# Attention and a feed-forward pair in one kernel: v times p of two head pairs in one run on TensorE, and a new order of work

## The chip, the cores and the metric

The kernel runs on 1 core of one Trainium2 chip. The metric is the device time of one launch in microseconds (us). The kernel before takes 998.44 us, the median of 3 runs (998.38 to 999.49).

## What is computed

Eight batches of eight heads, 576 tokens, head size 64, block-causal attention with blocks of 64 tokens; then a feed-forward layer with SiLU over all 4608 tokens:

```python
def _attn_ref(q, k, v):
    scores = 1/sqrt(64) * q @ k.T
    scores = where(pos_i // 64 >= pos_j // 64, scores, -1e9)
    scores = scores - max(scores)
    attn = exp(scores)
    attn = attn / (sum(attn) + 1e-9)
    return attn @ v

x = attn_out.transpose(0, 2, 1, 3).reshape(4608, 512)
h = x @ w_in                      # 512 x 2048
out = (h * sigmoid(h)) @ w_out    # 2048 x 512
```

All data are float32.

## The kernel before

**The order is written out.** A string, `ORDER`, lists some 4500 tokens, one for each step: `u20.scores`, `w3.bits:0`, `ffn`. The loop at L1196 calls the method that a token names, and each engine then runs its instructions in the order in which the tokens stand. Tile pools insert the waits. So where a step stands among the steps of its own engine decides when it can run.

**Names.** `a`, `b` (class First) are the first 64 query rows of all heads, `c0` to `c3` (Second) the next 64; `u0` to `u63` (Unit) are one head each, of the remaining 448 query rows. `w0` to `w15` are pieces of W_in, `o0` to `o15` pieces of W_out, `t0` to `t7` (Turned) pieces of W_out in the seven-product form below. `ffn` is the next half-step of x times W_in (ffn1), `keep` and `save` bring its result h through SBUF to DRAM. `i0` to `i71` (Item) read h back, apply SiLU and split it; `y0` to `y17` (Out) are the 18 output blocks of 256 rows, four items each. `warm:n` are matmuls of zeros. In `a`, `b` and `c`, `norm` divides p by its sum and `turn` transposes p on PE ahead of their `pv`.

**Precision.** Each float32 factor is split into a rounded fp32r part (`hi`, ScalarE) and the rest (`lo`, VectorE or GpSimd), and three fp32r matmuls make one product. Only v times p (`Unit.pv`, L800) is done with unsplit float32. Weights arrive as 64-bit words; `rebias` (ScalarE), `sign` (GpSimd, the first four W_in pieces) and `bits` (VectorE, through PSUM bank "C") turn them into float32.

**A unit.** `split_hi`, `split_q` and `split_k` (ScalarE and others) split q and k ahead of it. `scores` (L702) fills three of four PSUM banks. `max`, `gather`, `top`, `spread`, `wide` find and broadcast the row maximum, `sub` and `exp` make p. Units go in pairs: `pv` of the odd unit multiplies v of both heads with their p, one head to each half of PE's columns, ten matmuls in five widths into bank `U`. Then `inverse`, `mult` (U times the inverse sum), `x_hi`, `x_lo` make one 128-row piece of x. p has three buffers (`p{u.i % 3}`, L753).

**The stages.** From the start to some 100 us: `a`, `b`, `c` and the weights. To some 565 us: the units, with `ffn` half-steps between them on PE. Then the rest of `ffn`, while t3 to t7 are made. Last, the products `prod` of 18 blocks: seven half-size products in place of eight (`PRODUCTS`), added up by `Out.add` (L1143, VectorE) from four PSUM banks, which the next block's products fill again. t0 to t2 lie in the pool `ta` (NTA = 3) and are made among the units.

Of the kernel before, what the change touches and what calls it, by code (L numbers as in the profile page):

```python
# [72 lines left out]
c0.scores:0 b.back:0 b.turn:1 w5.rebias w1.lo w2.bits:0 w4.rebias ffn c0.max:0 b.back:1 w3.sign w2.bits:2 c0.exp:0 w9.load b.pv
w3.bits:0 c0.scores:1 w10.load all.mask b.hi:0 w3.bits:2 b.hi:1 ffn w2.hi c0.max:1 c3.load_v w3.hi w2.lo b.lo:0 c0.exp:1 b.lo:1
w4.bits:0 w3.lo ffn c0.sum w6.rebias c1.load w4.bits:1 w7.rebias c0.norm w4.bits:2 ffn keep w11.load w8.rebias w5.bits:0 w4.hi
save c0.turn:0 w5.bits:1 keep w4.lo c3.scores:0 w12.load c0.back:0 w5.bits:2 o1.rebias c0.turn:1 c3.max:0 w5.hi ffn save w6.bits:0
c0.back:1 w5.lo c3.exp:0 w6.bits:1 w13.load c0.pv w6.bits:2 c3.scores:1 c0.hi c1.load_v w7.bits:0 w6.hi ffn c0.lo w10.rebias
w14.load w6.lo c3.max:1 w9.rebias w7.bits:1 c3.exp:1 c1.scores:0 w7.bits:2 ffn c1.max:0 w15.load keep c3.sum c1.exp:0 save
w8.bits:0 c3.norm ffn w8.bits:1 w7.hi w8.bits:2 c1.scores:1 keep w7.lo w9.bits:0 c3.turn:0 w11.rebias save c1.max:1 w8.hi c2.load
ffn w9.bits:1 c3.back:0 w8.lo c1.exp:1 w9.bits:2 c3.turn:1 ffn w10.bits:0 c3.back:1 c1.sum w10.bits:1 w9.hi c1.norm c3.pv keep  # L80
w10.bits:2 w12.rebias ffn save w11.bits:0 w10.hi w9.lo w13.rebias w11.bits:1 c1.turn:0 o0.rebias w11.bits:2 ffn w10.lo c1.back:0
w12.bits:0 w11.hi w14.rebias c1.turn:1 w12.bits:1 w11.lo ffn c1.back:1 w12.bits:2 keep w13.bits:0 w15.rebias save c1.pv w12.hi
w13.bits:1 ffn w12.lo c1.hi c2.load_v w13.bits:2 c1.lo w13.hi c2.scores:0 w14.bits:0 keep w13.lo w14.bits:1 save ffn u0.load
c2.max:0 w14.bits:2 c2.exp:0 ffn w15.bits:0 w15.bits:1 w14.hi c2.scores:1 w15.bits:2 keep w14.lo ffn save c2.max:1 w15.hi u1.load
o0.bits:0 w15.lo all.staged c2.exp:1 ffn o0.bits:1 o0.bits:2 u0.split_hi ffn c2.sum o2.load o1.bits:0 c2.norm keep o1.bits:1
t0.hi:0 ffn save o1.bits:2 u0.split_q t0.hi:1 o3.load c2.turn:0 keep ffn u0.split_k c2.back:0 save c2.turn:1 ffn u2.load t0.x:0
c2.back:1 t0.x:1 c2.pv t0.hi:2 keep t0.x:2 u0.load_v ffn c2.hi save t0.lo:0 c3.hi u2.load_v c2.lo t0.hi:3 u3.load_v t0.lo:2 ffn
c3.lo u1.load_v t0.lo:3 u0.scores keep u0.max:0 t0.lo:1 save u0.max:1 ffn u1.split_hi u0.max:2 o2.rebias ffn u1.split_q u0.gather
o2.bits:0 o3.rebias u1.split_k u0.top ffn o2.bits:1 u0.spread u0.wide keep u3.load ffn u0.sub:0 u0.sub:1 save u0.exp:0 u1.scores
u0.sub:2 u0.exp:1 u0.exp:2 u1.max:0 ffn u1.max:1 u2.split_hi u0.add:0 u1.max:2 keep ffn u2.split_q u0.sums:0 u1.gather save  # L90
o2.bits:2 u0.add:1 u1.top ffn u1.spread o4.load o3.bits:0 u2.split_k u1.wide keep t1.hi:0 ffn u0.sums:1 save u1.sub:0 u4.load
t1.lo:0 u1.sub:1 u1.exp:0 u2.scores keep u1.sub:2 u1.exp:1 save u2.max:0 ffn u1.exp:2 u2.max:1 u3.split_hi u1.add:0 u2.max:2 u1.pv
u3.split_q u1.sums:0 u2.gather o3.bits:1 u2.top u3.split_k o3.bits:2 u2.spread ffn o5.load t1.hi:1 u2.wide u5.load u1.add:1
u2.sub:0 u2.sub:1 u3.scores t1.x:0 u2.exp:0 u4.load_v keep u3.max:0 u5.load_v u2.exp:1 save u1.sums:1 t1.x:1 ffn u4.split_hi
u3.max:1 t1.x:2 u3.max:2 t1.hi:2 ffn u4.split_q t1.hi:3 u2.sub:2 u3.gather u4.split_k ffn u1.sums_x u2.exp:2 u3.top u2.sums:0
u3.spread ffn u6.load u1.sums_g u2.add:0 u3.wide keep u3.sub:0 u2.add:1 u3.sub:1 save u4.scores u3.exp:0 keep u4.max:0 u1.sums_m
u3.exp:1 u2.sums:1 save ffn u5.split_hi u3.sub:2 u4.max:1 u5.split_q u3.exp:2 ffn u4.max:2 u3.add:0 ffn u1.inverse keep u4.gather
u1.mult save u3.add:1 u3.pv u4.top u3.sums:0 u4.spread u5.split_k u3.sums:1 u1.x_hi u4.wide u3.sums_x u4.sub:0 u7.load u1.x_lo
u3.sums_g u4.sub:1 u5.scores u4.exp:0 u6.load_v u4.sub:2 u3.sums_m u4.exp:1 u7.load_v u5.max:0 u4.exp:2 ffn u5.max:1 u6.split_hi
u4.add:0 u5.max:2 ffn keep u3.inverse u6.split_q u5.gather save ffn u5.top u3.mult u5.spread u4.add:1 u4.sums:0 u3.x_hi u5.wide  # L100
u6.split_k ffn keep u4.sums:1 save u5.sub:0 ffn u5.sub:1 u8.load u3.x_lo u5.exp:0 u5.sub:2 u5.exp:1 t1.lo:3 u6.scores u5.exp:2
u6.max:0 keep u5.add:0 u6.max:1 u5.pv save u7.split_hi u6.max:2 u5.add:1 u5.sums:0 u6.gather u7.split_q u5.sums:1 u6.top ffn
u5.sums_x u8.load_v u6.spread u7.split_k u9.load_v u5.sums_g u6.wide ffn u6.sub:0 u9.load u5.sums_m u6.sub:1 u6.exp:0 u7.scores
u6.sub:2 u6.exp:1 u6.exp:2 u7.max:0 t1.lo:1 u7.max:1 ffn keep u8.split_hi save u7.max:2 u6.add:0 ffn o5.rebias u5.inverse
u8.split_q u7.gather u5.mult ffn keep u7.top u6.add:1 u6.sums:0 u7.spread save u8.split_k ffn u5.x_hi u7.wide o4.rebias u6.sums:1
u7.sub:0 ffn u10.load u5.x_lo keep u7.sub:1 u7.exp:0 save u7.sub:2 u7.exp:1 t1.lo:2 u8.scores o4.bits:0 u7.exp:2 u8.max:0 u7.add:0
u7.pv u8.max:1 u9.split_hi u8.max:2 u7.add:1 u9.split_q u7.sums:0 u8.gather u7.sums:1 ffn u10.load_v u8.top u7.sums_x u9.split_k
u8.spread o4.bits:1 u11.load_v u7.sums_g u8.wide ffn u8.sub:0 keep u11.load u7.sums_m u8.sub:1 u8.exp:0 u9.scores save u8.sub:2
u8.exp:1 u9.max:0 u8.exp:2 ffn u9.max:1 u10.split_hi u8.add:0 u9.max:2 ffn u10.split_q keep u7.inverse u9.gather save u10.split_k
ffn u9.top u7.mult u9.spread u8.sums:0 u7.x_hi u9.wide ffn u12.load u7.x_lo keep u9.sub:0 u9.sub:1 save u9.exp:0 u8.add:1  # L110
u10.scores u9.sub:2 u9.exp:1 u10.max:0 u9.exp:2 u9.pv u10.max:1 u11.split_hi u10.max:2 u11.split_q u8.sums:1 u10.gather u9.sums:0
ffn u11.split_k u12.load_v u10.top o4.bits:2 u10.spread u13.load_v u10.wide t2.hi:0 ffn u13.load u9.add:0 keep u10.sub:0 u10.sub:1
u10.exp:0 save u9.add:1 u11.scores u10.sub:2 u10.exp:1 t2.lo:0 u11.max:0 u10.exp:2 ffn u9.sums:1 u12.split_hi u11.max:1 u10.add:0
ffn u11.max:2 keep u12.split_q save u9.sums_x u11.gather u10.sums:0 ffn u11.top u10.add:1 u9.sums_g o5.bits:0 u11.spread
u12.split_k ffn u10.sums:1 keep u11.wide u11.sub:0 save ffn u9.sums_m u14.load u11.sub:1 u11.exp:0 u12.scores u11.sub:2 u11.exp:1
u11.exp:2 u12.max:0 u12.max:1 ffn keep u11.add:0 u13.split_hi save u12.max:2 ffn u11.add:1 u9.inverse u12.gather u13.split_q ffn
# [1132 lines left out]
```

## Time and profile before

| | |
|---|---|
| median of 3 runs | 998.44 us |
| the profiled execution | 999.48 us |
| its span, from first to last instruction | 997.8 us |
| PE busy, weight loads busy | 987.2 us, 888.9 us |
| DVE, ACT, POOL busy | 768.4, 692.4, 616.0 us |
| granted TensorE clock | 1.00 |

PE is TensorE's matmul side and PEld its weight loads, DVE is VectorE, ACT ScalarE, POOL GpSimd, SP the queue that issues the DMAs. The profiled execution is 1.68 us longer than its span. A matmul's end in a trace is modelled, so a busy PE can still hide short gaps; starts are measured.

### The profile page before, as it was taken

How to read it: one execution, taken by the hardware profiler on the slowest of the kernel's cores; microseconds unless marked ns; L12 is line 12 of the kernel's file. 1: busy time of each engine (PE TensorE's matmuls, PEld its weight loads, DVE VectorE, ACT ScalarE, POOL GpSimd, SP SyncE). 2: the span in 40 equal slices, each digit the busy share in tenths (PEclk: the TensorE clock that was granted, in tenths of full speed). 3: DMA queues.
4: the chain of work that ended last, by engine and by line, in shares of the span. 5: the costliest groups of instructions: out<-in, count | busy, mean ns of one | idle time of the engine just before them, and what ended most of it. 6: DMA issues, size and time to landing. Idle time of an engine off the chain costs nothing. (4 is left out here: it accounts for less than half of the span.)

```text
span 997.8 us, 20716 instructions
## 1 busy us (share of the span) xinstructions
PE 987.2 (99%) x6936; PEld 888.9 (89%) x6936; DVE 768.4 (77%) x1969; ACT 692.4 (69%) x1555; POOL 616.0 (62%) x722
## 2 busy tenths in 40 slices
...
GB/s 351 387 195 187 170 144 154 151 145 149 159 147 147 149 159 142 146 166 144 145 149 148 76 208 216 179 164 154 127 128 132 145 128 127 128 126 143 135 43 44
DMA packets 109803, 155.51 MB, mean 156 GB/s; under 512 B 18560, under 2 KB 83072, under 8 KB 109696
## 3 DMA queue, kind: packets, MB, share of 16 engines
...
## 5 line engine op out<-in xcount | busy, mean ns | idle before, releaser
L1031 PE MATMUL h<-x,wi 128*128 128x448 f32 (+2 forms) x1968 | 422.4, 370 | 0.3 <-POOL wi L563 0.3
L1031 PEld LDWEIGHTS h<-x,wi 128*128 128x128 f32 x1968 | 357.3, 188 | 37.4 <-issue 0.9
L642 DVE TRANSPOSE_TENSOR_REDUCE Mx<-S 64x4 f32<-64x128 f32 (+4 forms) x384 | 130.4, 399 | 18.1 <-PE S L702 17.1
L755 ACT ACTIVATE p<-T 128x512 f32<-128x512 f32 (+1 forms) x192 | 114.2, 613 | 21.0 <-DVE T L745 16.1
L1037 ACT COPY g<-h 128x448 f32<-128x448 f32 (+1 forms) x160 | 86.4, 540 | 50.9 <-PE h L1031 36.0
L1096 POOL TENSOR_TENSOR x<-raw,x 128x512 fp32r<-128x512 f32 (+1 forms) x58 | 58.8, 1016 | 78.2 <-ACT x L1092 73.9
L1059 ACT ACTIVATE raw<-raw 128x1024 f32<-128x1024 f32 x72 | 76.3, 1061 | 41.7 <-DMA raw<-gdb 36.4
L1096 POOL TENSOR_TENSOR wi<-raw,wi 128x512 fp32r<-128x512 f32 (+1 forms) x56 | 56.7, 1017 | 77.6 <-ACT wi L1092 67.5
L761 POOL TENSOR_TENSOR pa<-p 128x448 f32<-128x448 f32 x64 | 73.5, 1149 | 48.4 <-ACT p L755 41.2
L683 POOL TENSOR_TENSOR qh<-qk,qh 64x576 fp32r<-64x576 f32 x64 | 91.4, 1428 | 5.0
L702 PE MATMUL S<-qh 128*128 128x448 f32 (+3 forms) x320 | 92.8, 303 | 0.0
L687 POOL TENSOR_TENSOR ql<-qk,qh 128x448 fp32r<-128x448 f32 x64 | 73.6, 1149 | 24.0 <-ACT qh L677 17.0
L677 ACT CAST qh<-qk 128x1024 fp32r<-128x1024 f32 x64 | 67.1, 1048 | 28.8 <-PE S L702 15.1
L805 PE MATMUL U<-p,v 128*64 128x448 f32 (+3 forms) x640 | 86.5, 416 | 0.0
L702 PE MATMUL S<-ql,qh 128*128 128x448 f32 (+3 forms) x320 | 83.9, 306 | 0.0
L805 PEld LDWEIGHTS U<-p,v 128*64 128x64 f32 x640 | 43.0, 137 | 42.3 <-issue 31.0
L748 DVE TENSOR_TENSOR T<-S,MR 128x384 f32<-128x384 f32 (+2 forms) x192 | 73.3, 408 | 0.0
L702 PEld LDWEIGHTS S<-ql,qh 128*128 128x128 f32 (+1 forms) x320 | 57.0, 178 | 6.5
L702 PEld LDWEIGHTS S<-qh 128*128 128x128 f32 (+1 forms) x320 | 56.8, 178 | 3.7
L764 POOL TENSOR_TENSOR pa<-pa,p 128x320 f32<-128x320 f32 x64 | 55.9, 873 | 2.5
L1096 POOL TENSOR_TENSOR gc<-raw,gc 128x512 fp32r<-128x512 f32 (+1 forms) x30 | 30.4, 1017 | 41.4 <-ACT gc L1092 33.5
L727 ACT COPY m<-m 32x14 f32<-32x14 f32 x192 | 38.7, 202 | 20.1 <-DVE m L723 18.0
...
## 6 DMA issues: line engine op xcount, KB each, us to landing
qk<-in_qk_dram SPq DMA_DIRECT2D x128, 256.0 KB, 3.8
gdb<-g SPq DMA_DIRECT2D x128, 224.0 KB, 2.3
...
wst<-in_moe_w_in_dram SPq DMA_DIRECT2D x16, 512.0 KB, 8.7
wst<-in_moe_w_out_dram SPq DMA_DIRECT2D x16, 512.0 KB, 4.4
...
```

Of the source, the lines that this page charges most:

```text
L642: nc.vector.tensor_reduce(out=out, in_=in_, axis=AX.X, op=op, apply_transpose=True)
L683: nc.gpsimd.tensor_tensor(out=u.qh[r, c], in0=u.raw[r, c], in1=u.qh[r, c], op=ALU.subtract)
L687: nc.gpsimd.tensor_tensor(out=u.ql, in0=u.raw[:, :NQ], in1=u.qh[:, :NQ], op=ALU.subtract)
L702: nc.tensor.matmul(u.ps(c, w, m), u.kk[r, j * P : j * P + m], q[r, q0 : q0 + w], start=qq == 0 and not (ROWS and seg in (2, 4)), stop=qq = ...
L748: nc.vector.tensor_tensor(out=u.T[:, c + 64 : c + w], in0=u.ps(c + 64, w - 64), in1=u.mb[:, q0 + 64 : q0 + w], op=ALU.subtract)
L755: nc.scalar.activation(u.p[:, c:e], u.T[:, c:e], AF.Exp, scale=SCALE)
L761: nc.gpsimd.tensor_tensor(out=u.pa, in0=u.p[:, :NQ], in1=u.p[:, 960 : 960 + NQ], op=ALU.add)
L805: nc.tensor.matmul(U[64 * e : 64 * e + 64, q0 : q0 + w], u.vv[:, e, j], z.p[:, c : c + w], start=n == 0, stop=n == 4)
L1031: nc.tensor.matmul(o, wi[wt][:, c, w], x_of(g, c, xt), start=c + k == 0, stop=c == CT - 1 and k == 2)
L1037: nc.scalar.copy(g, hs.pop(z)[:, :n])
L1059: nc.scalar.activation(u.raw, u.raw, AF.Silu)
L1096: e.tensor_tensor(out=u.goal(1, k), in0=u.source(k), in1=u.goal(0, k), op=ALU.subtract)
```

## The change

- `pv` of units from the ninth on (`u.double`) is called for every second pair and does two pairs one behind the other: the older pair (`units[u.i - 2]`) into bank `U`, its own into bank "C". p has five buffers from there, p3 and p4 in a new pool.
- NTA is 2: t2 is no longer made among the units but after them, and o4 and o5 with it. The pool of t0 and t1 is opened when the staging of W_in ends.
- For t2 to t7, `x:0`, `lo:1` and `lo:3` run on VectorE in place of GpSimd.
- `exp`, `sum`, `norm` of `a` and `b` go in two halves.
- w0 is the first DMA. The whole order is new.
- Switches that are off (BY_BIAS, RP, INPLACE, ROWS) change nothing; W_out's bits still go through bank "C".

```diff
-NTA = 3
+NTA = 2
+DOUBLE = 1
+INPLACE = 0
-LO_BY_VECTOR = ()
+LO_BY_VECTOR = (1, 3)
+X_BY_VECTOR = (0,)
...
 ORDER = """
-a.load b.load a.load_v w0.load b.load_v warm:10 a.scores w1.load w2.load a.max:0 a.sub:0 warm:3 b.scores c0.load a.max:1 a.sub:1
+w0.load a.load a.load_v b.load w1.load w3.load w0.rebias w0.sign b.load_v warm:16 a.scores w0.bits:0 w0.bits:2 w2.load w0.hi
...
 class Turned:
         def place(u):
             if u.d < NTA:
-                if u.d == 0:
-                    pools["ta"] = tc.alloc_tile_pool(name="ta", bufs=1, side="right")
                 t = pools["ta"].tile([P, 2, 7, 256], F32R, tag=f"ta{u.d}", name="ta")
...
         def x(u, k):
+            e = nc.vector if u.d >= NTA and k in X_BY_VECTOR else nc.gpsimd
...
         def lo(u, k):
-            e = nc.vector if k in LO_BY_VECTOR else nc.gpsimd
+            e = nc.vector if u.d >= NTA and k in LO_BY_VECTOR else nc.gpsimd
...
 class Unit:
+            u.double = DOUBLE and i >= 8
...
         def exp(u, k):
             if k == 0:
-                u.p = sp.tile([P, COLS], F32, tag=f"p{u.i % 3}", name="p")
+                n = u.i % 5 if u.double else u.i % 3
+                u.p = (pools["p"] if n > 2 else sp).tile([P, COLS], F32, tag=f"p{n}", name="p")
...
         def pv(u):
-            U = u.U = pU.tile([P, 512], F32, tag="U", name="U")[:, :NQ]
-            for n, (j, c, q0, w) in enumerate(SEG[i] for i in PV):
-                for e, z in enumerate((u.mate, u)):
-                    nc.tensor.matmul(U[64 * e : 64 * e + 64, q0 : q0 + w], u.vv[:, e, j], z.p[:, c : c + w], start=n == 0, stop=n == 4)
+            for y in (units[u.i - 2], u) if u.double else (u,):
+                U = y.U = (bank("C") if u.double and y is u else pU.tile([P, 512], F32, tag="U", name="U"))[:, :NQ]
+                for n, (j, c, q0, w) in enumerate(SEG[i] for i in PV):
+                    for e, z in enumerate((y.mate, y)):
+                        nc.tensor.matmul(U[64 * e : 64 * e + 64, q0 : q0 + w], y.vv[:, e, j], z.p[:, c : c + w], start=n == 0, stop=n == 4)
...
 class First(Early):
-        def exp(u):
-            nc.scalar.activation(u.p, u.p, AF.Exp, scale=SCALE)
+        def exp(u, k):
...
+                nc.scalar.activation(u.out(k), u.out(k), AF.Exp, scale=SCALE)
...
 class Phase:
         def staged(u):
             pools["stage"].release()
+            pools["ta"] = tc.alloc_tile_pool(name="ta", bufs=1, side="right")
+            if DOUBLE:
+                pools["p"] = tc.alloc_tile_pool(name="p", bufs=1, side="right")
```

PE among the units, before: the last score matmuls of a unit, v times p of one pair (L805, output bank U, the widths of `SEG`), and the half-step of `ffn` behind it.

```order
L702 MATMUL S_4524<-qh 64x64
L702 MATMUL S_4524<-ql,qh 64x64
L805 MATMUL U<-p,v 64x448 x4
L805 MATMUL U<-p,v 64x320 x2
L805 MATMUL U<-p,v 64x192 x2
L805 MATMUL U<-p,v 64x64 x2
L1031 MATMUL h<-x,wi_78 128x448 x2
L1031 MATMUL h<-x,wi_79 128x448
```

PE among the units, after (v times p is L816, `ffn` L1055); SC is bank "C".

```order
L711 MATMUL S_3705<-qh 64x64
L711 MATMUL S_3705<-ql,qh 64x64
L816 MATMUL U<-p,v 64x448 x4
L816 MATMUL U<-p,v 64x320 x2
L816 MATMUL U<-p,v 64x192 x2
L816 MATMUL U<-p,v 64x64 x2
L816 MATMUL SC<-p,v 64x448 x4
L816 MATMUL SC<-p,v 64x320 x2
L816 MATMUL SC<-p,v 64x192 x2
L816 MATMUL SC<-p,v 64x64 x2
L711 MATMUL S_3789<-qh 128x448
L711 MATMUL S_3789<-ql,qh 128x448
```

A second pair's ten matmuls now stand right behind the first's, and in the unit two further on none stand.

VectorE at the end of output block 10, before: L1143 are the sums of `Out.add`, which empty the PSUM banks of the block's products (S and c); L1079 and L1096 are `x` and `lo` of later items.

```order
L1143 TENSOR_TENSOR g_11387<-S_11150,s_11375 128x256
L1143 TENSOR_TENSOR u_11395<-S_11171,s_11375 128x256
L1143 TENSOR_TENSOR u_11397<-S_11171,u_11395 128x256
L1079 TENSOR_TENSOR h<-raw,h 128x256
L1143 TENSOR_TENSOR u_11407<-c_11195,u_11395 128x256
L1096 TENSOR_TENSOR wi_79<-S_11312,wi_78 128x2x256
L1096 TENSOR_TENSOR wi_79<-SC,wi_78 128x2x256
L1143 TENSOR_TENSOR g_11387<-c_11195,u_11397 128x256
L1143 TENSOR_TENSOR g_11435<-S_11171,u_11407 128x256
L1143 TENSOR_TENSOR g_11435<-S_11212,u_11407 128x256
```

The same place after (sums L1167, `x` L1103, `lo` L1120).

```order
L1167 TENSOR_TENSOR g_11386<-S_11157,s_11383 128x256
L1167 TENSOR_TENSOR u_11397<-S_11179,s_11383 128x256
L1103 TENSOR_TENSOR h<-raw,h 128x256
L1167 TENSOR_TENSOR u_11407<-S_11179,u_11397 128x256
L1103 TENSOR_TENSOR h<-h,raw 128x256
L1167 TENSOR_TENSOR u_11417<-c_11204,u_11397 128x256
L1167 TENSOR_TENSOR g_11419<-S_11179,u_11417 128x256
L1167 TENSOR_TENSOR g_11386<-c_11204,u_11407 128x256
L1103 TENSOR_TENSOR h<-h,raw 128x256
L1167 TENSOR_TENSOR g_11419<-S_11221,u_11417 128x256
L1120 TENSOR_TENSOR wi_79<-SC,wi_78 128x2x256
L1103 TENSOR_TENSOR h<-raw,h 128x256
```

The two `lo` that stood between the sums now stand behind the last of them.

GpSimd at the start, before: L528 is `sign` of w0 to w3, L563 `lo`, L855 `norm` of `a` (p) and `b` (T).

```order
L528 TENSOR_SCALAR wi_79<-wst 128x2x256
L855 TENSOR_TENSOR p_288<-p_288,rr 128x1024
L528 TENSOR_SCALAR wi_79<-wst 128x2x256
L563 TENSOR_TENSOR wi_79<-wm,wi_78 128x2x256
L855 TENSOR_TENSOR T<-T,rr 128x1024
L528 TENSOR_SCALAR wi_79<-wst 128x2x256
L563 TENSOR_TENSOR wi_79<-wm,wi_78 128x2x256
```

After (sign L537, lo L572, norm L946).

```order
L537 TENSOR_SCALAR wi_79<-wst 128x2x256
L572 TENSOR_TENSOR wi_79<-wm,wi_78 128x2x256
L946 TENSOR_TENSOR p_301<-p_301,rr 128x8x64 x2
L537 TENSOR_SCALAR wi_79<-wst 128x2x256 x2
L946 TENSOR_TENSOR T<-T,rr 128x8x64 x2
L537 TENSOR_SCALAR wi_79<-wst 128x2x256
L572 TENSOR_TENSOR wi_79<-wm,wi_78 128x2x256 x3
```

w0 is finished ahead of `a`'s norm, which goes in two halves.

## Rows read from the trace of the kernel before

**Rows 1.** Stretch, length, busy us: PE, PEld, DVE, ACT, POOL; clock, DMA, GB/s.

```profile
0.00:25.00 25.00, 21.41 (x376) 19.24 (x380) 14.27 (x25) 11.95 (x22) 13.21 (x16) 1.00 0.94 351
25.00:50.00 25.00, 24.12 (x275) 19.55 (x268) 22.11 (x38) 24.32 (x81) 15.17 (x18) 1.00 1.02 386
300.00:545.00 245.00, 245.00 (x1394) 207.68 (x1393) 216.29 (x642) 177.56 (x447) 185.95 (x240) 1.00 0.53 150
545.00:626.00 81.00, 81.00 (x419) 72.52 (x418) 40.57 (x86) 47.33 (x98) 51.66 (x60) 1.00 0.50 162
```

**Rows 2.** PE timeline, units 34 and 35: start us, length us, line, tile, count.

```profile
334.00 0.36 PE L702 MATMUL S<-qh 128*128 128x448 f32 x1
...
334.40 0.31 PE L702 MATMUL S<-qh 128*128 128x320 f32 x1
...
335.35 0.22 PE L702 MATMUL S<-ql,qh 128*64 128x64 f32 x1
335.50 2.70 PE L805 MATMUL U<-p,v 128*64 128x448 f32 x20
338.13 3.97 PE L1031 MATMUL h<-x,wi 128*128 128x448 f32 x18
341.94 0.37 PE L702 MATMUL S<-qh 128*128 128x448 f32 x1
...
343.31 0.22 PE L702 MATMUL S<-ql,qh 128*64 128x64 f32 x1
343.37 6.32 PE L1031 MATMUL h<-x,wi 128*128 128x448 f32 x30
349.52 0.36 PE L702 MATMUL S<-qh 128*128 128x448 f32 x1
```

**Rows 3.** PEld timeline: weight loads within that v times p.

```profile
336.31 0.14 PEld L805 LDWEIGHTS U<-p,v 128*64 128x64 f32 x2 [0.23 <-issue]
336.68 0.14 PEld L805 LDWEIGHTS U<-p,v 128*64 128x64 f32 x2 [0.23 <-issue]
```

**Rows 4.** POOL timeline at the start.

```profile
12.62 1.52 POOL L528 TENSOR_SCALAR wi<-wst 128x512 fp32r<-128x512 f32 x1 [11.03 <-DMA wst<-in_moe_w_in_dram]
14.11 1.90 POOL L855 TENSOR_TENSOR p<-p,rr 128x1024 f32<-128x1024 f32 x1
```

**Rows 5.** PE timeline at the start.

```profile
16.06 0.66 PE L862 MATMUL S<-ident,p 128*128 128x128 f32 x4 [0.27 <-POOL p L855]
...
32.59 0.66 PE L862 MATMUL S<-ident,MR 128*128 128x128 f32 x4
```

**Rows 6.** DMA issues of the first 25 us.

```profile
wst<-in_moe_w_in_dram SPq DMA_DIRECT2D x9, 512.0 KB, 9.5
```

**Rows 7.** Waits of the weight loads: total us, times, longest us.

```profile
PEld S L1108 <- DVE g L1143: 3.5, 7, 0.9
```

**Rows 8.** PE timeline where the products of block 11 begin.

```profile
854.02 1.69 PE L1108 MATMUL S<-ta,x 128*128 128x256 f32 x12 [0.72 <-DVE g L1143]
```

**Rows 9.** PE timeline after the units: last v times p, first product.

```profile
564.42 2.70 PE L805 MATMUL U<-p,v 128*64 128x448 f32 x20
...
626.73 1.71 PE L1108 MATMUL S<-ta,gc 128*128 128x256 f32 x12
```

**Rows 10.** ACT timeline after the units: rebias of o6, of o14 and o15.

```profile
574.53 0.67 ACT L518 ACTIVATE wraw<-wst 128x512 f32<-128x512 f32 x1 [1.74 <-DMA wst<-in_moe_w_out_dram]
...
614.48 1.38 ACT L518 ACTIVATE wraw<-wst 128x512 f32<-128x512 f32 x2 [0.35 <-POOL xs L620]
```

**Rows 11.** DVE timeline, units 34 and 35: first subtractions (L745), mult.

```profile
339.46 0.62 DVE L745 TENSOR_TENSOR T<-S,MR 128x448 f32<-128x448 f32 x1
...
347.59 0.59 DVE L809 TENSOR_TENSOR xu<-U,MR 128x448 f32<-128x448 f32 x1
348.10 0.61 DVE L745 TENSOR_TENSOR T<-S,MR 128x448 f32<-128x448 f32 x1
```

**Rows 12.** ACT timeline in unit 34: a split of queries.

```profile
336.01 1.05 ACT L677 CAST qh<-qk 128x1024 fp32r<-128x1024 f32 x1 [0.46 <-ACT g L1037]
```

More of the change, by code (lines that the diff above doesn't have):

```diff
@@ L73 @@
[L73 to L116, printed above, removed]
@@ L243 @@
-u63.max:0 u63.max:1 ffn keep u62.add:0 save u63.max:2 ffn u62.add:1 u61.inverse u63.gather ffn u63.top keep u62.sums:0 u62.sums:1
-u63.spread save u61.mult ffn u63.wide u61.x_hi u63.sub:0 u61.x_lo ffn keep u63.sub:1 u63.exp:0 save u63.sub:2 ffn u63.exp:1
-u63.exp:2 u63.sums:0 u63.pv u63.add:0 keep save u63.add:1 u63.sums:1 ffn u63.sums_x u63.sums_g ffn u63.sums_m ffn keep save
-u63.inverse ffn u63.mult ffn u63.x_hi keep u63.x_lo all.attended o6.load o7.load ffn save o6.rebias ffn keep o6.bits:0 save ffn
@@ L384 @@
[L384 to L386 removed]
+w0.load a.load a.load_v b.load w1.load w3.load w0.rebias w0.sign b.load_v warm:16 a.scores w0.bits:0 w0.bits:2 w2.load w0.hi
+a.max:0 c0.load w0.lo a.max:1 a.sub:0 a.sub:1 warm:10 b.scores a.exp:0 w4.load a.exp:1 a.sum:0 w8.load a.sum:1 a.norm:0 w1.rebias
@@ new lines @@
+b.max:0 w5.load a.norm:1 b.max:1 b.sub:0 w7.load w1.sign warm:14 a.turn:0 b.sub:1 b.exp:0 a.turn:1 w6.load a.back:0 b.sum:0
+o1.load a.back:1 w3.sign b.exp:1 warm:1 a.pv w1.bits:0 w2.rebias o0.load b.sum:1 b.norm:0 a.hi:0 c0.load_v a.hi:1 a.lo:0 b.norm:1
+a.lo:1 warm:7 c0.scores:0 w1.bits:2 w4.rebias w2.sign b.turn:0 c0.max:0 c3.load w1.hi b.turn:1 c0.exp:0 w1.lo w2.bits:0 ffn
+w2.bits:2 w3.rebias w10.load w2.hi w3.bits:0 c0.scores:1 b.back:0 w2.lo w3.bits:2 ffn b.back:1 w9.load w5.rebias c0.max:1 w3.hi
```

633 lines of the change are left out of this document (348 added, 285 removed).

## Prediction

> **What bounds the kernel now.** I read the busy time by stage first. In the stretch of the units from 300 to 545 us and in the stage behind them to 626 us PE is busy for the whole of it at a granted clock of 1.00, while VectorE, ScalarE and GpSimd are busy for 88% or less [rows 1]. The reader is to see two things: nothing but PE's own work sets the time there, so an edit counts only if it makes that work shorter, or leaves PE without work; and a modelled end can hide a short gap, so gaps have to be looked for between starts. Only the first 50 us show PE idle in that view, for 3.59 and 0.88 us [rows 1]. Then I read PE's timeline in two neighbouring units, for what an entry into v times p costs [rows 2, 3], then the waits of the weight loads, which name the one engine that PE waits for in the products [rows 7, 8], and last the starts of the three transitions [rows 4, 5, 9, 10].
>
> **v times p in doubles.** Counted from the two orders, 14 calls make two pairs and 4 make one, so 18 runs of these matmuls replace 32; PE's matmuls, columns and weights stay the same, and 14 entries and exits go. In unit 34 the last score matmul starts at 335.35 and v times p at 335.50, a step of 0.15; in unit 35, without v times p, ffn follows its last score matmul after 0.06 [rows 2]. So the entry costs 0.09. From the start of v times p to the next ffn are 2.63 us [rows 2]. Its loads come in steps of 0.37 us for a width of 448 (336.31 to 336.68) [rows 3]; the five widths, twice, sum to 2944 columns, which makes 2944 / 448 x 0.37 = 2.43. The rest, 0.20, is the run's start and end. As a cross-check, unit 34 lasts 7.94 us with 18 ffn matmuls and unit 35 lasts 7.58 with 30 [rows 2]; twelve of these at 0.205 (from 343.37 to 349.52 for 30) are 2.46, so v times p costs 2.82 in place, 0.39 over its streaming. Bounds per merged pair: 0.09, if only the entry goes, and 0.39, if all goes. I take 0.09 + 0.20 = 0.29, because the two starts on either side of the run measure just that. 14 x 0.29 = 4.0 us gained, between 1.3 and 5.5.
>
> The second pair lies in bank "C". Only W_out's bits of o2 to o5 want that bank among the units, and o4 and o5 now come after them. Its `mult` empties it, in a unit whose VectorE has room (216.29 of 245 us busy) [rows 1]. p lives longer, and has five buffers for it: the pairs of a double are written after the double before has read theirs, so no `exp` waits for PE. These are costed at nothing; without that cover each would cost what the slower rival below costs.
>
> **The start.** GpSimd's first `sign` waits for w0 until 12.62 and lasts 1.52 us; a's `norm` (1.90) comes behind it, and PE's first `turn` at 16.06 behind that [rows 4, 5]. Now w0 comes first, its `sign` and `lo` lie ahead of the softmax of `a`, and `norm` runs in halves, of which the first turn needs one. That takes up to 1.52 + 0.95 = 2.47 out of the chain. Against it, w0's 512 KB now pass SP's queue and the DMA engines ahead of a's q and k: at 351 GB/s that is 1.5 us [rows 1, 6]. The first turn then comes 1.0 us earlier. For `b`, half a norm (0.95) is taken out too, of which I count half, since w1 to w3 are worked on in between. Together 1.5 us. Bounds: nothing, if the DMA engines (busy 94% of the time) [rows 1] simply make `a` as late as the rest is earlier; and 4.5, all of PE's idle time there [rows 1].
>
> **The products.** The weight loads wait for the sums of `Out.add` in 7 places, 3.5 us together, 0.9 at most [rows 7]; at block 11 it is 0.72 [rows 8]. These are block ends at which the order puts `lo` of later items ahead of the sums that empty the banks, as shown above for block 10. In the new order the sums of y2 to y13 stand ahead of them, as they do in the blocks of before that show no wait; y0, y1 and y14 keep another order. I leave 1.2 us for those (two waits of up to 0.72 and less), so 2.3 are gained; bounds 3.5, and a loss of 0.5, if a displaced `lo` makes a product late instead.
>
> **W_out between units and products.** t2, o4 and o5 move behind the units. Among the units this buys nothing, since PE has no gap there. Behind them six t's are made in place of five, on ScalarE, GpSimd and VectorE, while PE has ffn left: v times p at 564.42 to the first product at 626.73 is 62.3 us [rows 9], with 49 half-steps of 1.22 between. By the new order 53 half-steps and a double lie there, 53 x 1.22 + 5.1 = 69.6. In before, four t's pass from the rebias at 574.53 to that at 614.48, 9.99 each [rows 10]. Three of seven heavy steps of each t move from GpSimd to VectorE, which is busy for 40.57 of 81 us there [rows 1]; at an estimated 8 us per t, with before's head of 10.1 and tail of 12.2 [rows 9, 10], 10.1 + 5 x 8 + 12.2 = 62.3 lies under 69.6. Costed at nothing; without that cover it is the first rival. The DMA queue is used to half there (0.50) [rows 1], and the later loads of o4 and o5 go beside work.
>
> **Sum.** 4.0 + 1.5 + 2.3 = 7.8 us. The profiled execution took 999.48 (997.8 of span, 1.68 around it), 1.04 above the median; it becomes 991.7, and the median 998.44 - 7.8 = 990.6. A measurement of this kernel can tell about 0.2%, 2 us, from no change.
>
> **Rivals.** *The t's become the bound.* If sharing saves nothing and a t still takes 9.99, then 10.1 + 50 + 12.2 = 72.3 against a cover of 69.6: PE stands still for 2.7 us, and the time is 993.3. For it: GpSimd is busy for 51.66 of the 81 us [rows 1]. Against: the moved steps were its own. Chance 0.10. The Trainium skill (GPSIMD Engine Reference, 1. Specifications) says that GpSimd shares its SBUF interfaces with VectorE and that VectorE instructions with two SBUF inputs contend with it; some of the moved steps have two. By that rule the sharing would buy less, as this rival has it; no run so far shows it.
>
> *Only the entry goes.* If the 0.20 behind the streaming belongs to each pair's own widths and not to the run, the gain is 14 x 0.09 = 1.3 and the time 993.3. For it: the steps for the narrow widths may be longer than their columns, which two rows of one width can't show [rows 3]. Chance 0.12. The Trainium skill (TensorE: Matmul & The Clock Gate, Step-by-step: what each phase is for; TensorEngine Tiling (Array Packing), Key Properties) has the last column need some 128 cycles to drain and each change of tiling mode drain the engine: as an estimate from these pages, 28 changes of 53 ns each, 1.5 us. The measured row of 0.09 fits it at the entry; the 0.20 behind is more than it explains.
>
> *Start and products give nothing.* Queues fill up again elsewhere: 998.44 - 4.0 = 994.4. Chance 0.10.
>
> *Slower: VectorE's chain in the unit of a double.* There PE has scores and 5.06 us of v times p, and then the scores of the next unit, with no ffn between. Scores take 1.50 [rows 2], so the next begin after 6.56 instead of 7.94, and want their second bank (0.40 on) after 6.96. That bank is emptied by the first subtraction of the maximum: in unit 34 it ends at 340.08, 6.08 after the unit's first score, in unit 35, where `inverse` and `mult` lie ahead, at 348.71, 6.77 after [rows 2, 11]. The margin is 0.2 to 0.9 us. If one split of queries (1.05 on ScalarE) [rows 12] falls ahead of the copies in that chain, the subtraction is 0.8 late by the worse of these, in each of 14 doubles: 11.2 us, 990.6 + 11.2 = 1001.8. It decides from 7.8 / 14 = 0.56 us per double. Against: the order has `mult` behind the subtraction in most of these units, and the splits where they were. Chance 0.06.
>
> **How the numbers follow.** The forecast, 990.6, has the remaining 0.62. Its own terms reach from 985 (5.5 + 4.5 + 3.5) to 997.6 (1.3 + 0 - 0.5), with the ends unlikely all at once; 987.0 to 996.0 holds most of it and the first three rivals, and leaves out the fourth and the corners. Faster by over 0.2% means under 996.4: all but a corner of the forecast and of the third rival, 0.85. Within 0.2%: 0.08. Slower: 0.07, the last rival and what is like it.
>
> **What would show it.** Right: 14 runs of 40 matmuls of v times p whose second half starts within 0.05 us of the end of the first's streaming, with 5.1 us to the next matmul; no wait of PE for VectorE in these units; the first turn before 15.2 and c0's (32.59 before) [rows 5] before 31.5; waits of the weight loads for the sums at 1.5 us or less; PE without a gap behind the units. Wrong: matmuls of scores that wait for VectorE in units of a double, a gap ahead of the first product, or a start no earlier than before.

## The result and the profile after

The changed kernel takes 990.47 us, the median of 4 runs (990.21 to 992.26), where the kernel before takes 998.97 in 4 runs beside it: a ratio of 0.9916, 95% interval 0.9904 to 0.9928. The forecast was 990.6, in a range of 987.0 to 996.0.

The same stretches of the changed kernel's profile as in [rows 1], with the columns as there (PE, PEld, DVE, ACT, POOL; clock, DMA, GB/s):

```profile
0.00:25.00 25.00, 18.40 (x332) 16.37 (x332) 14.86 (x30) 11.54 (x26) 13.57 (x18) 0.93 0.95 353
25.00:50.00 25.00, 25.00 (x268) 20.96 (x267) 21.96 (x37) 23.61 (x75) 14.29 (x18) 0.93 1.02 383
300.00:545.00 245.00, 245.00 (x1412) 209.59 (x1411) 225.29 (x671) 184.78 (x465) 194.89 (x248) 1.00 0.54 150
545.00:626.00 81.00, 81.00 (x425) 72.83 (x424) 51.22 (x90) 48.10 (x97) 35.74 (x46) 1.00 0.60 195
```

PE is as full as before in the units and behind them. VectorE is busy for 51.22 us from 545 to 626 us where it was 40.57, GpSimd for 35.74 where it was 51.66: the moved steps of the t's. In the first 50 us the granted clock is 0.93. This one execution, 992.26 us, is the slowest of the four. Shorter stretches show where the clock stood at or near the lower of its two levels (1.2 of 2.4 GHz) for a part of the time:

```profile
4.00:6.00 2.00, 0.72 (x7) 0.53 (x5) 0.00 (x0) 0.62 (x1) 0.95 (x1) 1.00 1.02 385
6.00:8.00 2.00, 0.97 (x48) 0.84 (x52) 1.37 (x2) 0.00 (x0) 0.56 (x1) 1.00 1.05 395
8.00:10.00 2.00, 2.00 (x44) 1.88 (x35) 1.41 (x4) 0.62 (x1) 1.18 (x1) 0.53 1.01 410
10.00:12.00 2.00, 2.00 (x66) 1.88 (x68) 1.86 (x4) 1.23 (x2) 0.09 (x1) 0.62 1.03 399
...
20.00:25.00 5.00, 3.61 (x36) 3.00 (x32) 2.84 (x5) 3.19 (x12) 2.52 (x2) 1.00 1.05 391
25.00:30.00 5.00, 5.00 (x77) 4.44 (x79) 4.22 (x8) 4.88 (x16) 2.57 (x2) 0.66 1.04 398
```

From 8 to 12 us it is near half (0.53, 0.62), after four microseconds with PE busy for 0.72 + 0.97; from 25 to 30 us it is at 0.66, after five with 3.61. So the changed kernel was run again, for a profile without these falls (first experiment), and the start is read from that one.

**v times p.** PE's timeline at one double of the changed kernel (start us, length us, line, tile, count), against [rows 2]:

```profile
377.25 0.22 PE L711 MATMUL S<-ql,qh 128*64 128x64 f32 x1
377.40 2.70 PE L816 MATMUL U<-p,v 128*64 128x448 f32 x20
379.93 2.65 PE L816 MATMUL SC<-p,v 128*64 128x448 f32 x20
382.51 0.47 PE L711 MATMUL S<-qh 128*128 128x448 f32 x1
382.82 0.36 PE L711 MATMUL S<-ql,qh 128*128 128x448 f32 x1
```

The entry is as before, 0.15 from the last score. The second pair starts 2.53 us behind the first, where 2.63 passed to the next matmul before. The first score matmul behind takes a step of 0.31 (382.51 to 382.82); between the first two of a unit it is 0.20 or 0.21 elsewhere (in that of unit 34, 334.00 to 334.40 for two [rows 2]). All 14 doubles are alike to 0.01 us: 5.115 us from the first matmul to the score or ffn behind, where two single runs take 2 x 2.632. So the second pair adds 5.115 - 2.632 = 2.483 us, which I take as the streaming of one pair.

**VectorE's chain** in the unit of that double in the profile without the falls (next section; times there are some 1.6 us earlier), PE first, then VectorE:

```profile
374.27 0.36 PE L711 MATMUL S<-qh 128*128 128x448 f32 x1
...
375.77 2.70 PE L816 MATMUL U<-p,v 128*64 128x448 f32 x20
...
381.40 0.31 PE L711 MATMUL S<-qh 128*128 128x320 f32 x1
```

```profile
379.65 0.63 DVE L754 TENSOR_TENSOR T<-S,MR 128x448 f32<-128x448 f32 x1
```

The first subtraction ends 6.01 us after the unit's first score, and the second bank is wanted 7.13 after it: 1.1 us of room. In the ten doubles with scores right behind it is 0.8 to 1.1 us; the tightest room among the units with doubles, 0.34 us, lies in a unit that follows a double (from 410.32 us). No row of the waits has PE waiting for VectorE among these units, nor for the sums of `Out.add` in the products (3.5 us in [rows 7]), and none has `exp` waiting for PE there.

### The profile page after: what moved, and what is told of

Its sections match the earlier page's. It is cut to its first block, busy times and chain, and to the rows that moved or that the text cites. A ratio compares the mean times of both kernels' runs of the same rounds, so it can differ in the third digit from the quotient of the medians.

```text
span 990.5 us, 20760 instructions
## 1 busy us (share of the span) xinstructions
PE 979.7 (99%) x6928; PEld 887.2 (90%) x6928; DVE 785.7 (79%) x1993; ACT 691.6 (70%) x1557; POOL 596.4 (60%) x706
## 4 chain that ended last, share of the span: by engine, by line
PE 95%; DMA 2%; POOL 1%; DVE 1%; ACT 0%; issue 0%; SPq 0%; DVEq 0%; POOLq 0%
PE h L1055 40%; PE S L1132 26%; PE c L1132 10%; PE S L711 9%; PE U L816 5%; PE SC L816 4%; DMA wst<-in_moe_w_in_dram 1%; DMA qk<-in_qk_dram 1%; PE S L996 1%; POOL wi L572 0%; PE S L1027 0%; PE S L873 0%; DVE SC L554 0%; DVE wm L560 0%; POOL MR L866 0%
## 5 line engine op out<-in xcount | busy, mean ns | idle before, releaser
L1055 PE MATMUL h<-x,wi 128*128 128x448 f32 (+2 forms) x1968 | 419.2, 369 | 1.4 <-POOL wi L572 0.9
L1055 PEld LDWEIGHTS h<-x,wi 128*128 128x128 f32 x1968 | 358.9, 189 | 36.9 <-POOL wi L572 1.1
L1061 ACT COPY g<-h 128x448 f32<-128x448 f32 (+1 forms) x160 | 86.4, 540 | 39.8 <-PE h L1055 19.7
L1120 POOL TENSOR_TENSOR x<-raw,x 128x512 fp32r<-128x512 f32 (+1 forms) x58 | 58.8, 1017 | 80.5 <-ACT x L1116 73.3
L1120 POOL TENSOR_TENSOR wi<-raw,wi 128x512 fp32r<-128x512 f32 (+1 forms) x56 | 56.7, 1017 | 75.7 <-ACT wi L1116 73.5
L757 DVE TENSOR_TENSOR T<-S,MR 128x128 f32<-128x128 f32 (+2 forms) x192 | 73.8, 412 | 0.0
L1132 PE MATMUL S<-tb,x 128*128 128x256 f32 x450 | 58.8, 283 | 0.0
L1120 POOL TENSOR_TENSOR gc<-raw,gc 128x512 fp32r<-128x512 f32 (+1 forms) x30 | 30.5, 1020 | 44.2 <-ACT gc L1116 40.5
L1132 PEld LDWEIGHTS S<-tb,x 128*128 128x128 f32 x450 | 56.1, 192 | 0.0
L654 DVE STREAM_TRANSPOSE MR<-m 128x448 f32<-128x448 f32 x64 | 40.2, 628 | 19.2 <-ACT m L736 18.8
```

Of the source, the lines that this page charges most:

```text
L757: nc.vector.tensor_tensor(out=u.T[:, c + 64 : c + w], in0=u.ps(c + 64, w - 64), in1=u.mb[:, q0 + 64 : q0 + w], op=ALU.subtract)
L1055: nc.tensor.matmul(o, wi[wt][:, c, w], x_of(g, c, xt), start=c + k == 0, stop=c == CT - 1 and k == 2)
L1061: nc.scalar.copy(g, hs.pop(z)[:, :n])
L1120: e.tensor_tensor(out=u.goal(1, k), in0=u.source(k), in1=u.goal(0, k), op=ALU.subtract)
L1132: nc.tensor.matmul(o, quarter(u.g[a], j)[:, P * e : P * e + P], quarter(turned[d].g[b], TORDER[FACTOR[pr]]), start=u.q == 0 and i % 2 == 0 ...
```

## The experiments

**1. The changed kernel again,** with no edit.

> The changed kernel itself, unaltered, for a profile of an execution in which TensorE's granted clock does not fall at the start (it was 0.93 over the first 50 us in the one profiled, whose span was 990.5 us where the three others had 988.5 to 988.8). Theory: the fall cost that execution some 1.8 us, so an undisturbed profile has a span of 988.6 +- 0.3 and its first 50 us hold some 1.5 us more of the kernel's matmuls than in the kernel before. Rival: the start gains nothing and the other runs differ elsewhere; then the stage from 0 to 100 us is no better than before in an undisturbed profile either. Median 990.4 by both.

Measured: 991.23 (990.59 to 991.65), and a profile with the clock at 1.00 in all of these stretches and a span of 988.9. Its start:

```profile
0.00:25.00 25.00, 19.43 (x334) 17.46 (x336) 15.00 (x31) 11.77 (x27) 13.57 (x18) 1.00 0.95 350
25.00:50.00 25.00, 25.00 (x275) 20.83 (x276) 21.78 (x37) 24.54 (x77) 15.78 (x19) 1.00 1.03 392
```

```profile
9.52 0.69 DVE L863 TENSOR_REDUCE m<-S 128x8 f32<-128x512 f32 x1 [1.94 <-PE U L917]
```

```profile
4.61 1.51 POOL L537 TENSOR_SCALAR wi<-wst 128x512 fp32r<-128x512 f32 x1 [3.02 <-DMA wst<-in_moe_w_in_dram]
...
13.39 2.05 POOL L946 TENSOR_TENSOR p<-p,rr 128x512 f32<-128x512 f32 x2 [3.74 <-DVE rr L943]
```

```profile
15.50 0.65 PE L873 MATMUL S<-ident,p 128*128 128x128 f32 x4 [0.16 <-POOL p L946]
...
22.12 1.21 PE L1055 MATMUL h<-x,wi 128*128 128x256 f32 x8
24.25 0.74 PE L1055 MATMUL h<-x,wi 128*128 128x256 f32 x4 [0.92 <-POOL wi L572]
...
31.72 0.66 PE L873 MATMUL S<-ident,MR 128*128 128x128 f32 x4
```

```profile
21.58 0.69 ACT L527 ACTIVATE wm<-wst 128x512 f32<-128x512 f32 x1 [1.62 <-DMA wst<-in_moe_w_in_dram]
```

(VectorE, GpSimd, PE and ScalarE, one fence each.) GpSimd no longer waits until 12.62 for w0 [rows 4] but has its `sign` done at 6.12. In its place it waits 3.74 us for a's inverse sums, since a's first maximum starts at 9.52, where it was 6.90 before. The first `turn` (15.50) starts behind both halves of `norm` (13.39 to 15.44). c0's turn is at 31.72 against 32.59 [rows 5]. VectorE in the kernel before, for comparison:

```profile
6.90 0.69 DVE L852 TENSOR_REDUCE m<-S 128x8 f32<-128x512 f32 x1 [5.91 <-PE U L906]
...
12.99 0.26 DVE L922 RECIPROCAL rr<-U 128x16 f32<-128x16 f32 x1
```

There a's inverse sums were ready at 13.25, so w0's `sign`, which let `norm` start at 14.11, held it for 0.86 us only. Counted over the trace, the matmuls but the zeros that had started by 100 us have 1536 columns more than in the kernel before; at the 0.205 us of an ffn matmul of 448 columns [rows 2] that is some 0.7 us. In the profile with the falls they have 2048 fewer, 0.9 us. So the falls cost some 1.6 us, which is also the difference of the two spans, and the start gains some 0.7 us in place of the 1.5 expected of it.

**2. The start alone.**

```diff
-ORDER_BEFORE[:238] + ORDER_BEFORE[238:]
+ORDER_AFTER[:244] + ORDER_BEFORE[238:]
```

(`ORDER_BEFORE` and `ORDER_AFTER` are the tokens of the two orders; both cuts lie at 76 us, with the same steps ahead of them, but that the softmax of `a` and `b` is in halves and a few zeros are gone.)

> The kernel before with the new order up to 76 us only (w0 first, softmax of a and b in halves, new places up to o0), all behind it as before. Theory: 1.5 us of the whole gain come from here: 997.3 where the kernel before has 998.8. Rival: nothing comes from here, 998.8 (what a comes late by, its rest is earlier); or more than 3 us, if the clock's fall is what usually stands there.

Measured: 997.67 (996.75 to 1000.08 in 11 runs) where before has 998.71 (997.13 to 999.89 in 21); the ratio of the comparison is 0.9995 (0.9986 to 1.0004): 0.5 us less, between 1.4 less and 0.4 more (the medians are 1.04 apart). 1.5 us is just outside that range, and no gain at all is inside it.

**3. The products alone.**

```diff
-ORDER_BEFORE[:2961] + ORDER_BEFORE[2961:]
+ORDER_BEFORE[:2961] + ORDER_AFTER[2953:]
```

(The cut is at i6.prod:1, with the same steps behind it in both.)

> The kernel before with the new order from the product i6.prod:1 on, all ahead of it as before. Theory: the waits of TensorE for the sums (3.5 us of weight loads in 7 places, 1.6 of matmuls) go: 2.3 to 3.5 us less, 995.5 to 996.5. Rival: only the named waits of the matmuls (1.6) count, 997.2; or the waits return at another block end, 998.8.

Measured: 996.03 beside 998.71, 0.9972 (0.9962 to 0.9982): 2.7 us less, between 1.8 and 3.8. Of [rows 7] this is left in its view of the waits:

```profile
PEld S L1108 <- DVE g L1143: 0.2, 1, 0.2
```

**4. The pairs apart.**

```diff
 def pv(u):
     for y in (units[u.i - 2], u) if u.double else (u,):
         ...
+        if u.double and y is u:
+            part(1)
```

(`part(1)` issues the first matmul of the next half-step of `ffn`, which then goes on from its second.)

> The changed kernel with one matmul of ffn (the first of the next half-step) between the two pairs of each double, 14 times; nothing else moves. Theory: each run of v times p costs an entry and an exit whatever its length, 0.345 us together by the starts in the two traces (0.09 ahead, 0.149 within, 0.106 at the matmul behind): 14 x 0.345 = 4.8 us more than the changed kernel, 995.2. Rival 1: only the entry is the run's own, 14 x 0.09 = 1.3 more, 991.7. Rival 2: the doubles gain through something else (buffers of p, fewer waits on VectorE), and one matmul between changes nothing: 990.4.

Measured: 996.05 (995.4 to 996.22) on the chip on which the changed kernel took 991.23: 4.8 us more, 0.344 for each of 14. That is the theory's number, and neither rival's. Its trace has the cost in place, at the same double:

```profile
378.52 2.70 PE L818 MATMUL U<-p,v 128*64 128x448 f32 x20
381.15 0.47 PE L1065 MATMUL h<-x,wi 128*128 128x448 f32 x1
381.56 2.70 PE L818 MATMUL SC<-p,v 128*64 128x448 f32 x20
```

The pair ahead takes 2.63 again (2.483 within a run), and the one ffn matmul takes a step of 0.403 where 0.205 is usual: 0.149 + 0.198 = 0.347. What in a run makes the cost was not taken apart: v times p differs from its neighbours both in its 64 columns of weights and in its unsplit float32.

**5. The middle alone.**

```diff
-ORDER_AFTER[:244] + ORDER_AFTER[244:2953] + ORDER_AFTER[2953:]
+ORDER_BEFORE[:238] + ORDER_AFTER[244:2953] + ORDER_BEFORE[2961:]
```

(The softmax of `a` and `b` is whole again with it.)

> The start (to 76 us) and the products (from i6.prod:1 on) in the order of before, with the softmax of a and b whole; between them the change: doubles, t2, o4 and o5 behind the units, three steps of a t on VectorE. Theory: only the 14 merged runs count, 4.8 us, and all else in this part is covered: 993.9 where before has 998.7. Rival: moving t2, o4 and o5 out of the units gains too, over 5.8 us, under 992.9; or the transition costs something, 995 and more.

Measured: 992.82 beside 998.3, 0.9944 (0.9931 to 0.9957), 5.6 us less, between 4.3 and 6.9. 4.8 lies in it. But the products of this run, in the order of before, wait for the sums of `Out.add` in one place, 1.0 us, where [rows 7] has seven and 3.5 us: the middle part takes waits out of the products too, so the terms of the three parts overlap and can't simply be added. Against it, the products' plain steps are longer by some 1.5 us in all (next section).

**6. The t's steps back on GpSimd.**

```diff
-LO_BY_VECTOR = (1, 3)
-X_BY_VECTOR = (0,)
+LO_BY_VECTOR = ()
+X_BY_VECTOR = ()
```

> The changed kernel with x:0, lo:1 and lo:3 of t2 to t7 back on GpSimd; the order as it is. Theory by the prediction's sum: six t's at 9.99 us each need 72.3 us where 69.6 of TensorE's work cover them, so a gap of 2.7 us stands ahead of the first products, 993.7. Rival: the queue of t's runs ahead of need or is quicker than 9.99 each, and nothing changes, 991.0. Rival 2: in this order GpSimd's steps wait for one another, over 5 us more.

Measured: 995.31 (994.97 to 996.32), where the changed kernel has 990.5 to 991.2 in its three sets of runs, on other chips: 4.1 us or more. PE's timeline, and GpSimd's at the first and the sixth `x:0`:

```profile
601.51 7.57 PE L1055 MATMUL h<-x,wi 128*128 128x448 f32 x36 [0.49 <-ACT g L1061]
609.80 14.62 PE L1055 MATMUL h<-x,wi 128*128 128x448 f32 x66 [0.73 <-ACT g L1061]
```

```profile
565.75 1.30 POOL L624 TENSOR_TENSOR xs<-wraw 128x512 f32<-128x512 f32 x1 [2.05 <-DVE wraw L560]
...
614.97 1.29 POOL L624 TENSOR_TENSOR xs<-wraw 128x512 f32<-128x512 f32 x1 [1.14 <-PE h L1055]
```

A t takes (614.97 - 565.75) / 5 = 9.84 us, nearly the 9.99 of before. But the gap is not ahead of the first product: `ffn` waits for a PSUM bank of h, which ScalarE empties by its copy to g (L1061). Two of these waits show in the matmuls above; the weight loads wait in eight places, for 4.3 us in all, where the changed kernel has one of 0.2:

```profile
PEld h L1055 <- ACT g L1061: 4.3, 8, 1.1
```

At the two places above, the copy stands behind a rebias (L527) and a cast of the t's (L638) that wait for GpSimd:

```profile
599.29 0.67 ACT L527 ACTIVATE wraw<-wst 128x512 f32<-128x512 f32 x1 [1.71 <-POOL xs L628]
...
600.94 0.51 ACT L1061 COPY g<-h 128x448 f32<-128x448 f32 x1
...
608.70 0.62 ACT L638 CAST wi<-xs 128x512 fp32r<-128x512 f32 x1 [2.14 <-POOL xs L628]
609.23 0.53 ACT L1061 COPY g<-h 128x448 f32<-128x448 f32 x1
```

The undisturbed profile of the changed kernel has the first and the sixth `x:0` and a `lo` on VectorE, and two `x:1` (L626) on GpSimd:

```profile
565.43 0.69 DVE L624 TENSOR_TENSOR xs<-wraw 128x512 f32<-128x512 f32 x1
566.09 0.69 DVE L643 TENSOR_TENSOR tb<-wraw,tb 128x512 fp32r<-128x512 f32 x1
...
610.77 0.69 DVE L624 TENSOR_TENSOR xs<-wraw 128x512 f32<-128x512 f32 x1
```

```profile
566.25 1.12 POOL L626 TENSOR_TENSOR xs<-wraw,xs 128x256 f32<-128x256 f32 x1 [2.79 <-PE h L1055]
...
575.98 0.73 POOL L626 TENSOR_TENSOR xs<-wraw,xs 128x256 f32<-128x256 f32 x1 [3.28 <-DVE xs L624]
```

A t takes 9.07 here, not the 8 that I had estimated, and PE goes from ffn to the first product without a wait. The step `x:1` of GpSimd takes 1.12 us beside the `lo` on VectorE at 566.09, and 0.73 with no such neighbour, 0.4 us of the sharing given back. The Trainium skill (GPSIMD Engine Reference, 1. Specifications) has GpSimd share its SBUF interfaces with VectorE, with contention where a VectorE instruction has two SBUF inputs, as this `lo` has. The trace agrees in part: of the six `x:1`, three began behind the start of a `lo` and took 1.12; one, at 584.02, began ahead of a `lo` and took 0.74, and there the `lo` took 0.98 where it takes 0.69.

**7. a's loads ahead of w0's.**

```diff
-w0.load a.load a.load_v ... a.scores w0.bits:0 w0.bits:2 ... w0.hi a.max:0 ... w0.lo
+a.load w0.load a.load_v ... a.scores ... a.max:0 ... a.norm:1 w0.bits:0 w0.bits:2 w0.hi w0.lo
```

> The changed kernel with the load of w0 behind that of a's q and k (one place of SP's queue), and w0's bits, hi and lo behind a's norm; the rest of the order as it is. Theory: w0's 512 KB ahead of a make a's first maximum 2.6 us later than before (9.52 against 6.90), which eats what the shorter chain behind gains; with a first, the first turn comes at 13.5 to 14.5 where the changed kernel has 15.50, and 0.5 to 1.0 us are gained at the end, 990.2. Rival: the start is bound by the sum of bytes (DMA engines busy all the time to 50 us), and the order of two loads changes nothing at the end, 991.0; or w0's later pieces hold up the first ffn, 992.

Measured: 991.92 (991.69 to 992.65) where experiment 8 on the same chip has 991.25: not faster. a's `norm` ran from 10.53 to 12.58, but the turn came at 16.14, because b's scores and 28 zeros stand ahead of it on PE; the scores waited for their tiles, and the zeros took 3.25 us, where 28 zeros take 1.85 in experiment 1 (from 13.49). The granted clock was 0.74 from 12 to 14 us and 0.50 from 14 to 16, after PE was busy for 0.69 of the four microseconds from 8 to 12, so part of the late turn is the clock's:

```profile
10.53 2.05 POOL L946 TENSOR_TENSOR p<-p,rr 128x512 f32<-128x512 f32 x2 [0.97 <-DVE rr L943]
```

```profile
12.96 3.25 PE L845 MATMUL h<-zero 128*64 128x64 f32 x28
16.14 0.74 PE L873 MATMUL S<-ident,p 128*128 128x128 f32 x4
```

**8. norm cut by what a turn reads.**

```diff
-u.engine.tensor_tensor(out=u.out(k), in0=u.out(k), in1=u.spread(u.rr[:, k]), ...)
+z = u.part(k)...
+u.engine.tensor_tensor(out=z, in0=z, in1=r, ...)
```

> The changed kernel with the halves of norm cut by what a turn reads (four heads, both parts) in place of by the part, so that the first turn needs one half only. In the changed kernel's trace the first turn (15.50) starts behind the second half (15.44), not behind the first. Theory: the first turn comes 1.0 us earlier, 14.5, and at the end 0 to 0.5 us of it are left, 990.8. Rival: all of the 1.0 us is left, 990.0; or the halves cost more in this shape, 991.5.

Measured: 991.25 (990.52 to 992.77). The first turn now starts ahead of the second half's end,

```profile
14.08 2.08 POOL L948 TENSOR_TENSOR p<-p,rr 128x512 f32<-128x512 f32 x2 [4.24 <-DVE rr L943]
```

```profile
15.24 0.66 PE L873 MATMUL S<-ident,p 128*128 128x128 f32 x4
```

1.16 us after the first half began, where it was 2.11 in experiment 1. But `norm` itself began 0.69 later in this execution, so the turn is only 0.26 earlier, and the first ffn is at 22.14, against 22.12. More telling are the profiles with w0's load first, nine of them with this one: their first turn lies between 13.94 and 15.50 us, their first ffn between 21.59 and 22.28, and not in the same order.

**9. w4's rebias behind w1's hi.**

```diff
-... w1.bits:2 w4.rebias w2.sign ... w1.hi b.turn:1 ...
+... w1.bits:2 w2.sign ... w1.hi w4.rebias b.turn:1 ...
```

> The changed kernel with one step moved: the rebias of w4 behind w1's hi on ScalarE, where it stood ahead of it and waited 1.62 us for its DMA (at 21.58 in the undisturbed trace). Theory: that wait holds w1's hi, lo and with them ffn's second half-step (TensorE waits 0.92 us at 24.25), so 0.5 to 0.9 us less than the changed kernel's 991.2: 990.5. Rival: the next link is as late (DMA engines are busy all the time), and nothing changes at the end, 991.2.

Measured: 990.78 (990.12 to 991.62), ratio to before 0.9925 (0.9912 to 0.9937). PE's wait for w1's `lo` goes as expected, from 0.92 (the row at 24.25 in experiment 1) to

```profile
23.22 0.73 PE L1055 MATMUL h<-x,wi 128*128 128x256 f32 x4 [0.22 <-POOL wi L572]
```

**10. All of b behind a's turn.**

```diff
-... warm:10 b.scores a.exp:0 ... b.max:0 ... warm:14 a.turn:0 b.sub:1 b.exp:0 a.turn:1 ... a.pv ...
+... warm:24 a.exp:0 ... a.turn:0 a.turn:1 ... b.scores ... b.max:0 ... a.pv b.sub:1 b.exp:0 ...
```

> As the step before, and a's load ahead of w0's, with all of b's scores and softmax behind a's turn on each engine. In the run with a's load first a's norm ended at 12.58 but its turn came at 16.14, because b's scores stood ahead of it on TensorE and waited for their DMA. Theory: now a's turn comes at 12.7 to 13.5, the first ffn at 20 in place of 22.1, and 1 to 2 us are gained at the end, 989.5. Rival: c's tiles and W_in's pieces come no earlier, as the DMA engines are busy without a break, and the end moves by less than 0.5 us, 990.7 or more.

Measured: 992.85 (991.64 to 993.62), slower than experiment 9 on the same chip by 2.1 us. The turn comes at 12.86 as expected, and the first ffn at 24.62, later than in any other run:

```profile
12.86 1.11 PE L873 MATMUL S<-ident,p 128*128 128x128 f32 x4 [3.28 <-POOL p L946]
...
21.53 1.09 PE L996 MATMUL S<-qk 64*64 64x128 f32 x16 [1.53 <-DVE x L967]
23.77 1.09 PE L873 MATMUL S<-ident,T 128*128 128x128 f32 x8 [1.15 <-POOL T L946]
24.62 1.19 PE L1055 MATMUL h<-x,wi 128*128 128x256 f32 x8
```

```profile
12.00:25.00 13.00, 9.46 (x179) 8.42 (x180) 8.25 (x17) 6.26 (x12) 8.42 (x7) 0.74 1.05 392
```

Ahead of the first ffn PE now waits twice: c0's scores (21.53) for the lower part of a's x (L967), which stands behind b's steps on VectorE, and b's turn (23.77) for b's `norm`. But the granted clock is 0.74 from 12 to 25 us, after PE had no matmul from 10 to 12; experiment 9's profile has 0.86 up to 12 us and 1.00 from there to 25. The falls of the first profile, 0.57 from 8 to 12 and 0.66 from 25 to 30, take as much from the clock (4 x 0.43 + 5 x 0.34 = 3.4, and 13 x 0.26 = 3.4), and cost some 1.6 us. So how much of the 2.1 us is the order's and how much the clock's is not separated; what is shown is that the earliest turn of all brought no earlier ffn.

**11 and 12. The kernel of experiment 9 and the changed kernel on one chip.**

> The kernel with w4's rebias moved behind w1's hi once more, now on one chip beside the changed kernel (next run), since 990.78 on one chip and 991.23 on another can't be set against each other. Theory: TensorE's wait for w1's lo falls from 0.92 to 0.22 and 0.4 us of that are left at the end: median 0.2 to 0.7 under the changed kernel's. Rival: no difference.

> The changed kernel itself beside it: median 990.5 to 991.2, 0.2 to 0.7 above the run before by the theory, level with it by the rival.

Measured: 990.48 (990.3 to 990.84) and 990.80 (990.49 to 991.12). The 0.3 us have the sign and size that were expected, but the two sets of four overlap: not settled. Both are faster than the kernel before by over 8 us.

## Why the prediction was right, and where it was not

The time was right to 0.1 us, which is luck in part: the three sets of runs of the changed kernel have medians from 990.47 to 991.23, one term was too large and others too small, and a cost that the sum does not have came in.

- *v times p in doubles:* forecast 4.0, measured 4.8 (experiment 4). The mechanism held, and no merged pair met a wait. The term was mis-sized because I stopped the sum at the start of the next matmul. What a run costs beside its streaming is 0.09 at its entry, 2 x 2.632 - 5.115 = 0.149 inside (I had 0.20, with the streaming at 2.43 in place of 2.483), and 0.106 in the step of the matmul behind it (0.31 for 0.20), 0.345 in all. The last part lay in the cross-check (0.39 over the streaming) and I didn't take it. The rival of the entry alone (1.3) is excluded. The estimate of 53 ns for a change, worked out from two pages of the Trainium skill (TensorE: Matmul & The Clock Gate, Step-by-step: what each phase is for; TensorEngine Tiling (Array Packing), Key Properties), makes 0.106 for the two of a run, under a third of what a run costs here.
- *The start:* forecast 1.5, measured 0.5 (nothing to 1.4, experiment 2), some 0.7 by the columns counted at 100 us. The steps of the sum failed, though their balance for the first turn did not. `sign` lay in the chain for 0.86 us, not 1.52. "The first turn needs one" half of `norm` is wrong, for `norm` is cut across the heads that a turn reads. w0's load ahead of `a` costs not 1.5 us but 1.1 to 2.6 at a's first maximum (7.96 to 9.52 in the nine profiles, 6.90 before). What the sum left out is that `a`'s softmax in halves, no longer behind b's maximum, is shorter: from the first maximum to the first turn are 5.98 us (9.52 to 15.50) where 9.16 were. So the turn came 0.4 to 2.1 us earlier where I had 1.0, 0.56 in experiment 1. For `b` nothing came: its `norm` ends at 20.68, before at 20.64. And the gain at the turn does not arrive. The first ffn stands on PE behind c0's scores, which wait for the lower part of a's x (0.44 us in experiment 1, 1.65 in experiment 9, where the turn is earliest of the nine), and ffn's next half-step waits for w1. c0's turn gains 0.87. The bound of nothing was as near as the value taken.
- *The products:* forecast 2.3, measured 2.7 (1.8 to 3.8). The mechanism held; I had left 1.2 us of the waits for y0, y1 and y14, and in the trace 0.2 (experiment 3) or none is left.
- *W_out behind the units:* costed at nothing, and right up to the first product. The cover is real: from the double at 551.03 to the first product at 620.70 are 69.7 us, where I had 69.6. It needs the three steps on VectorE: without them 4.1 us are lost (experiment 6), where the rival had 2.7. The rival's place was wrong, since PE stalls in ffn, by way of ScalarE's copies, before the cover ends; and my 8 us a t were 9.07. In the products the middle part of the change has a cost that I overlooked. The mean step from one product matmul to the next, steps over 0.16 us left out, is 119.4 ns in the kernel before and in experiments 2 and 3, and 120.0 in the changed kernel and in experiment 5; those that read `tb` go from 118.7 to 119.9. Over 3024 matmuls that is some 1.5 us. Why is not shown; the steps on VectorE are not it, since experiment 6 has the longer steps without them.
- *The slower rival* had the chain right, and the room is 0.8 to 1.1 us in these doubles where I had 0.2 to 0.9.

Of the signs, the 14 runs with 5.115 us to the next matmul, the waits and the first product came as forecast. The second half of a run starts 0.10 us behind the 2.43 of streaming where I allowed 0.05, and in experiment 1 the first turn (15.50) and c0's (31.72) missed their 15.2 and 31.5.

The terms as measured make 4.8 + 0.5 + 2.7 = 8.0 us; the ratio of 0.9916 (0.9904 to 0.9928) is 8.4 of 998.97, between 7.2 and 9.6. In the traces of before and of experiment 1 the first product comes 6.03 us earlier (626.73 to 620.70), of which the doubles have 4.83, and from the first to the last product matmul pass 363.85 us in place of 366.66, 2.81 less. There the waits that are gone were worth more, some 4.2 us with the longer step (0.22 us for 0.12) behind each, and the longer steps took some 1.5 back.
